# Layer one's outward products in 512 and 384 tokens, a cut in the middle, and a margin in the scheduler

## The chip, the cores and the metric

The kernel runs on one core of a Trainium2 chip. The metric is the device time of one execution in microseconds (us); lower is better. Before the change three runs gave 1051.30, 1053.89 and 1055.59 us, so the median is 1053.89 us.

## The reference

Sigmoid attention feeds two feed-forward layers over 1792 tokens (4 batches of 448), with 768 channels and 2048 hidden values:

```python
scores = scale * np.matmul(q, k.transpose(0, 1, 3, 2)) - np.log(S)   # 4 x 12 heads x 448 x 64
attn = 1.0 / (1.0 + np.exp(-scores))
x = np.matmul(attn, v)                       # to (1792, 768)

h = x @ w_in                                 # layer one: 768 -> 2048
g = np.maximum(h, 0.0) ** 2
x = g @ w_out                                # 2048 -> 768

h = x @ w_in2                                # layer two
g = np.maximum(h, 0.0) + alpha * np.minimum(h, 0.0)
out = g @ w_out2
```

## The kernel before

A first stage computes the attention (lines 290 to 480). The change does not touch it; its end is at about 159 us in the trace. What follows are the two layers, and everything below is about them.

**Units.** A layer's work is cut into units `(layer, p, fp)`: `p` is one of two pairs of batches (a pair is `PAIR = 896` tokens, side 0 the first 448, side 1 the last 448), and `fp` one of eight blocks of 256 hidden values (two halves `j` of 128). There are 16 units per layer, 32 in all, and they run one after the other. I number them 0 to 31; units 0 to 15 are layer one. The trace shows a unit every 27 to 30 us.

**Split numbers.** A float32 value is held as a high part and a low part (type fp32r), and each product of two such values takes three matmuls: high x high, high x low, low x high.

**A unit's inward half** (`product`, `add_inward`) computes the hidden values from x. Seven products `k = 0..6` of sums of blocks take the place of eight; each is nine matmuls of 128 x 448 into one PSUM bank of three (`BANK`). The first matmul of `k = 0` is cut in two at a column that goes through 32, 64, ... 416 with the unit's number, so the unit has 64 inward matmuls. VectorE (DVE) and ScalarE (ACT) take each bank out: DVE adds it to a running sum (L667), ACT applies the activation and writes the high part of g, DVE subtracts to get the low part (L659). Side 1 of g comes from `k = 3, 4`, side 0 from `k = 5, 6`.

**A unit's outward half** (`out_product`, `add_outward`) multiplies g with w_out. In layer one an output is a channel block `c` (six) by a side `t` (two); the weights stand in the array and 448 tokens of g stream past them: 12 outputs x 2 halves `j` x 3 = 72 matmuls of 448. Two outputs of one side make a pair, which fills one of the two double banks `two[0]`, `two[1]`; side 1 comes first (`for t in (1, 0)`). When a pair is done, DVE adds its 2 x 448 columns to the accumulator `acc` in SBUF (L727; for `fp == 0` ACT copies them instead, L725). A pair can start only when the pair before the last has been taken out. In layer two g stands in the array and 384 channels of w_out stream: 84 matmuls of 384.

**Other work.** DVE, ACT and GpSimd (POOL) also split the weights (L241, L630), sum and split x for the next layer (L258, L262, L265: x sums, high parts, low parts) and turn the float64 weights into float32 words (L191, L193, L203). SyncE (SP) starts the DMAs.

**What sets the order.** All work of the two layers is given as jobs to a planner (`Plan`): engine, estimated duration, what it reads and writes, and whether it uses the port that DVE and POOL share (`port=True`). `run` plays the jobs through a model of the engines and hands each engine's instructions out in that order; on the chip every engine keeps to it. TensorE's (PE's) order is fixed as written. Every other job has a due time, worked out backwards from the PE job that needs it. When an engine is free, `choose` takes the earliest due job that is ready, except that it waits for a job `s` that is due earlier and will be ready before the candidate's end, if the candidate's end falls after `due[s]`.

Of the kernel before, what the change touches and what calls it, by code (L numbers as in the profile page):

```python
# [16 lines left out]
P = 128  # L17


class Plan:  # L20
# [3 lines left out]


    HOP = 0.10
    AFTER_OWN = {"ACT": 0.12, "POOL": 0.05}
    TAIL = {"PE": 0.17, "DVE": 0.085, "ACT": 0.095, "POOL": 0.04}

# [16 lines left out]
    def run(self):  # L46
        jobs, n = self.jobs, len(self.jobs)
        after = [[] for _ in jobs]
        for j, job in enumerate(jobs):
            for i in job[3]:  # L50
                after[i].append(j)

        def length(j):
            return jobs[j][1] if jobs[j][0] != "SP" else jobs[j][5] / 0.28e6 + 2.0

        at, due, pe = 0.0, [0.0] * n, [j for j in range(n) if jobs[j][0] == "PE"]
        for j in pe:
            due[j] = at
            at += jobs[j][1]
        for j in reversed(range(n)):  # L60
            late = min((due[s] - self.HOP for s in after[j]), default=at + 50.0) - length(j) - self.TAIL.get(jobs[j][0], 0.0)
            due[j] = min(due[j], late) if jobs[j][0] == "PE" else late
        left = [len(job[3]) for job in jobs]
        ready = [0.0] * n
        engines = ("PE", "DVE", "ACT", "POOL", "SP")
        free = dict.fromkeys(engines, 0.0)
        waiting = {e: [] for e in engines}
        next_pe = 0
        port_free = dma_free = 0.0
        for j in range(n):  # L70
            if not left[j]:
                waiting[jobs[j][0]].append(j)
        order = []

        def begin(j, t):
            t = max(t, ready[j])
            return max(t, port_free) if jobs[j][4] else t

        def choose(e):
            queue = waiting[e]  # L80
            if e == "PE":
                queue = [j for j in queue if j == pe[next_pe]]
            if not queue:
                return None
            t = max(free[e], min(begin(j, free[e]) for j in queue))
            now = sorted((j for j in queue if begin(j, free[e]) <= t + 1e-9), key=lambda j: due[j])
            soon = [j for j in queue if begin(j, free[e]) > t + 1e-9]
            for j in now:
                end = t + jobs[j][1]
                if not any(due[s] < due[j] and begin(s, free[e]) < end and end > due[s] for s in soon):  # L90
                    return t, j
            s = min(soon, key=lambda j: begin(j, free[e]))
            return begin(s, free[e]), s

        while len(order) < n:
            t, j, e = min((*c, e) for e in engines if (c := choose(e)))
            engine, us, emit, before, port, size = jobs[j]
            waiting[e].remove(j)
            if e == "PE":
                next_pe += 1  # L100
            free[e] = t + us
            end = t + us + self.TAIL.get(e, 0.0)
            if port:
                port_free = t + us
            if e == "SP" or size:
                dma_free = max(dma_free, t + 0.1) + size / 0.28e6
                end = dma_free + 2.0
            order.append((t, j))
            for s in after[j]:
                left[s] -= 1  # L110
                ready[s] = max(ready[s], t + us + self.AFTER_OWN.get(e, 0.0) if jobs[s][0] == e and e != "SP" else end + self.HOP)
                if not left[s]:
                    waiting[jobs[s][0]].append(s)
        self.span = free["PE"]
        for t, j in sorted(order):
            jobs[j][2]()
# [3 lines left out]
def fused_kernel(ctx: ExitStack, tc: tile.TileContext, q, k, v, w1i, w1o, w2i, w2o, alpha, out):  # L120
# [124 lines left out]
    def values_of(p):  # L245
        return acc[p].rearrange("p (c t s) -> p c t s", c=NC, t=2)
# [23 lines left out]
    with tc.manual_schedule():  # L270
# [231 lines left out]
        OPERAND = (0, 4, 3, 5, 6, 1, 2)  # L502
        HIGH, LOW = ((0, 0), (0, 1)), ((1, 0),)
        CELL = 64
        CUT = 32

        def product(n, k):

            ps = hb[BANK[k]][:, :S]
            at_col = [0, CUT * (1 + n % (S // CUT - 1)), S] if k == 0 else [0, S]  # L510
            for c in range(KH):
                at = OPERAND[k] * HALF + c * P
                for i, (wp, xp) in enumerate(((0, 0), (0, 1), (1, 0))):
                    ends = at_col if (c, i) == (0, 0) else [0, S]
                    for a, e in zip(ends, ends[1:]):
                        nc.tensor.matmul(ps[:, a:e], W[:, wp, at:at + P], X[k][:, xp, c, a:e], start=(k < 3 and c == 0 and i == 0 and a == 0), stop=(c == KH - 1 and i == 2), skip_group_check=True)  # L516

# [6 lines left out]
        def sides(n, o):  # L524

            if UNITS[n][0] == 0:
                return [o[1]]
            return [t for t in range(2) if o[0] * P < (t + 1) * S and (o[0] + 1) * P > t * S]

        def out_product(n, o, ps, j, ways, begin, end):  # L530

            for i, (gi, wi) in enumerate(ways):
                if UNITS[n][0] == 0:
                    c, t = o
                    ops = WO[j][:, wi, c * P:(c + 1) * P], G[j][:, gi, t * S:(t + 1) * S]
                else:
                    m, e = o
                    ops = G[j][:, gi, m * P:(m + 1) * P], WO[j][:, wi, e * HALF:(e + 1) * HALF]
                nc.tensor.matmul(ps, *ops, start=(begin and i == 0), stop=(end and i == len(ways) - 1), skip_group_check=True)  # L539

        def part_of(n, os):
            layer, p, fp = UNITS[n]
            if layer == 0:
                c, t = os[0]
                cells = [((c + i) * 2 + t) * S // CELL + k for i in range(2) for k in range(S // CELL)]
                return values_of(p)[:, c:c + 2, t], cells
            m = os[0][0]
            return acc[p][:, m * DM:(m + 1) * DM].rearrange("p (e c) -> p e c", e=2), [m * DM // CELL + k for k in range(DM // CELL)]

# [26 lines left out]
        def pool(cols):  # L576
            return 0.13 + 0.0023 * cols

        PE_IN, PE_OUT = 0.2027, (0.2027, 0.1740)
        BYTES = 4 * P  # L580

        def cells_of(p, name, c):
# [78 lines left out]
        def add_inward(n):  # L661

            def bank(b):
                return hb[b][:, :S]

            def total(to, b, other, key, other_key):
                add("DVE", dve(S), lambda: nc.vector.tensor_add(to, bank(b), other), [("h", b), other_key], [key])  # L667

            for k in range(7):
                reads = [("w", OF_STEP[k], i) for i in range(2)] + [key for c in range(KH) for key in x_keys(k, c)]  # L670
                b = BANK[k]
                add("PE", 9 * PE_IN, lambda k=k: product(n, k), reads, [("h", b)])
                if k == 0:
                    add("ACT", act(S), lambda: nc.scalar.activation(e21, bank(0), AF.Copy), [("h", 0)], ["e21"])
                elif k == 1:
                    total(e12, 1, e21, "e12", "e21")
                elif k == 2:
                    total(e22, 2, e21, "e22", "e21")
                elif k == 3:
                    total(e22, 1, e22, "e22", "e22")  # L680
                    add_hidden(n, e22, "e22", e22, "e22", 1, 1)
                elif k == 4:
                    total(e12, 2, e12, "e12", "e12")
                    add_hidden(n, e12, "e12", e12, "e12", 0, 1)
                elif k == 5:
                    add_hidden(n, bank(0), ("h", 0), e11, "e11", 0, 0)
                else:
                    total(e21, 1, e21, "e21", "e21")
                    add_hidden(n, e21, "e21", e21, "e21", 1, 0)
# [3 lines left out]
        def add_outward(n):  # L693

            layer, p, fp = UNITS[n]
            size = HALF if layer else S
            pairs = []
            for os in outputs(n):
                pairs.append((os, at_pair[0] % 2))
# [2 lines left out]
            def keys(o, j, ways):  # L702
                return [("g", j, t, gi) for gi, _ in ways for t in sides(n, o)] + [key for _, wi in ways for key in ([("wo", j, 0)] if wi == 0 else [("wo", j, 1, e) for e in range(2)])]

            def products(os, b, i, j, ways, begin, end):
                add("PE", len(ways) * PE_OUT[layer], lambda: out_product(n, os[i], two[b][:, i, :size], j, ways, begin, end), keys(os[i], j, ways), [("o", b)])

            for os, b in pairs[:2]:
                for i in range(2):
# [1 line left out]
            for at, (os, b) in enumerate(pairs):  # L711
# [8 lines left out]
                        products(os, b, i, 1, HIGH + LOW, False, True)  # L720
                part, cells = part_of(n, os)
                cells = [("acc", p, cell) for cell in cells]
                both = two[b][:, :, :size]
                if fp == 0:
                    add("ACT", act(2 * size), lambda part=part, both=both: nc.scalar.activation(part, both, AF.Copy), [("o", b)], cells)  # L725
# [89 lines left out]
```

## Time and profile before

| | |
|---|---|
| three runs | 1051.30, 1053.89, 1055.59 us |
| profiled execution | 1051.43 us, of which the trace's span is 1049.6 us |
| PE busy | 1039.2 us, 99% of the span, 5639 matmuls |
| DVE, ACT, POOL busy | 746.3 us (71%), 595.6 us (57%), 256.6 us (24%) |
| inward matmuls (L516) | 2048, of which 64 are the halves of cut ones |
| outward matmuls (L539) | 1152 of 448 columns (layer one), 1344 of 384 (layer two) |

PE's busy time counts a matmul from its start to its modelled end, and matmuls overlap: one of 448 columns is listed with 366 ns, but the next starts about 203 ns after it. So the pace is read from starts: the start of a run of equal matmuls, the start of the next run, and the count between them. In the timeline view consecutive instructions of one line are merged into one row (with the shape of the first), and a row carries in brackets how long the engine stood idle before it and what ended that.

### The profile page before, as it was taken

What the parts mean: (1) busy time and instruction counts of PE and PEld (TensorE: products, weight loads), DVE (VectorE), ACT (ScalarE), POOL (GpSimd) and SP (SyncE); (2) the same over time, 40 slices, a digit from 0 to 9 for tenths busy, and PEclk for the clock granted to TensorE, in tenths of its full rate; (3) what the DMA queues carried; (4) which work ended last, traced back from release to release, by engine and by line L of the source; (5) the groups of instructions that cost most, each with busy time, mean ns of one, the idle gap of its engine ahead of it and who ended that gap; (6) DMA issues with size and microseconds to landing.
All of it is one profiled execution on the core that took longest, in us unless ns stands there. A gap on an engine that the chain in (4) does not pass through costs nothing.

```text
span 1049.6 us, 14891 instructions
## 1 busy us (share of the span) xinstructions
PE 1039.2 (99%) x5639; PEld 916.3 (87%) x5639; DVE 746.3 (71%) x990; ACT 595.6 (57%) x933; POOL 256.6 (24%) x229
## 2 busy tenths in 40 slices
PE   9999999999999999999999999999999999999998
PEld 6555548999999989899999998999999999999998
DVE  5555986698777785877777867777667656777765
ACT  4567777776666557556665675444443463343432
POOL 0001233263321152633111324432111211111110
PEclk9999999999999999999999999999999999999999
DMA  7577737666665676757677844333115611111103
GB/s 148 143 192 195 202 113 290 212 234 219 216 215 184 255 271 224 253 182 241 229 253 233 323 155 145 110 97 112 57 50 212 225 61 61 61 61 60 51 10 106
DMA packets 126007, 174.78 MB, mean 167 GB/s; under 512 B 55536, under 2 KB 98800, under 8 KB 124272
## 3 DMA queue, kind: packets, MB, share of 16 engines
q1 hardware_dynamic: 123440, 172.59, 50.6%
q10 hardware_dynamic: 2496, 1.25, 0.4%
q8 instruction: 44, 0.72, 0.3%
q14 instruction: 27, 0.22, 0.1%
HBM read 123.87 MB, written 49.94 MB: 166 GB/s over the span
## 4 chain that ended last, share of the span: by engine, by line
PE 94%; DVE 4%; issue 1%; DMA 1%; ACT 0%; SPq 0%; DVEq 0%; ACTq 0%
PE o L539 42%; PE h L516 39%; PE av L371 5%; PE sc L351 4%; DVE acc L727 1%; PE tp L318 1%; PE scr L361 1%; PE av L379 1%; DVE wi L241 1%; PE tp L321 1%; DVE x L265 1%; DMA raw<-in_moe_w_in_dram 1%; DVE g L659 0%; PE busy L395 0%; PE tp L319 0%
## 5 line engine op out<-in xcount | busy, mean ns | idle before, releaser
L516 PE MATMUL h<-x,wi 128*128 128x448 f32 (+2 forms) x2048 | 417.5, 363 | 0.5 <-DVE c L667 0.5
L516 PEld LDWEIGHTS h<-x,wi 128*128 128x128 f32 x2048 | 380.5, 188 | 32.2 <-DVE c L667 1.2
L539 PE MATMUL o<-g,wo 128*128 128x448 f32 x1152 | 238.4, 366 | 1.2 <-DVE acc L727 1.2
L539 PE MATMUL o<-wo,g 128*128 128x384 f32 x1344 | 237.0, 335 | 2.1 <-DVE g L659 1.6
L539 PEld LDWEIGHTS o<-wo,g 128*128 128x128 f32 x1344 | 233.6, 188 | 3.9 <-DVE g L659 2.3
L539 PEld LDWEIGHTS o<-g,wo 128*128 128x128 f32 x1152 | 216.0, 188 | 21.0 <-DVE acc L727 2.5
L630 POOL TENSOR_TENSOR wo<-words_o,wo 128x384 fp32r<-128x384 f32 x128 | 129.6, 1042 | 415.7 <-ACT wo L633 413.8
L727 DVE TENSOR_TENSOR acc<-o,acc 128x768 f32<-128x768 f32 (+1 forms) x182 | 184.5, 1016 | 62.8 <-PE o L539 62.4
L667 DVE TENSOR_TENSOR c<-h,c 128x448 f32<-128x448 f32 x160 | 99.5, 622 | 129.3 <-PE h L516 125.5
L633 ACT ACTIVATE wo<-words_o 128x768 fp32r<-128x768 f32 x64 | 50.7, 839 | 155.0 <-PE o L539 128.0
L659 DVE TENSOR_TENSOR g<-c,g 128x448 fp32r<-128x448 f32 x128 | 82.4, 652 | 15.2 <-ACT c L649 12.0
L353 ACT ACTIVATE a<-sc,bias 128x896 f32<-128x896 f32 x72 | 69.1, 1004 | 35.6 <-PE av L371 22.6
L265 POOL TENSOR_TENSOR stage<-acc,stage 128x448 fp32r<-128x448 f32 x36 | 45.3, 1260 | 160.9 <-ACT stage L262 160.9
L237 ACT ACTIVATE wi<-sums 128x768 fp32r<-128x768 f32 x64 | 53.5, 838 | 51.2 <-PE h L516 48.3
L191 ACT ACTIVATE raw<-raw 128x768 f32<-128x768 f32 x64 | 57.7, 904 | 37.0 <-DMA raw<-in_moe_w_out_dram 27.0
L241 DVE TENSOR_TENSOR wi<-sums,wi 128x768 fp32r<-128x768 f32 x64 | 65.4, 1023 | 10.3 <-ACT wi L237 9.4
L258 POOL TENSOR_TENSOR acc<-acc 128x448 f32<-128x448 f32 x40 | 58.4, 1465 | 10.1 <-DMA acc<-late 8.3
L371 PE MATMUL av<-a,v 128*64 128x448 f32 x288 | 59.4, 548 | 0.0
L193 ACT ACTIVATE raw<-raw 128x768 int32<-128x768 uint32 x64 | 57.2, 898 | 0.0
L655 ACT ACTIVATE pos<-c 128x448 f32<-128x448 f32 x48 | 27.7, 578 | 50.4 <-DVE c L667 49.7
L241 DVE TENSOR_TENSOR wi<-words_i,wi 128x768 fp32r<-128x768 f32 (+1 forms) x64 | 52.6, 823 | 3.5 <-ACT wi L237 3.1
L657 DVE SCALAR_TENSOR_TENSOR c<-c,nal,pos 128x448 f32<-128x448 f32 x64 | 44.4, 693 | 9.1 <-ACT c L656 8.9
(75 smaller groups left out, 850.3 us busy)
## 6 DMA issues: line engine op xcount, KB each, us to landing
raw<-in_moe_w_in_dram SPq DMA_DIRECT2D x32, 768.0 KB, 5.9
raw<-in_moe_w_out_dram SPq DMA_DIRECT2D x32, 768.0 KB, 5.3
kept_x<-stage SPq DMA_DIRECT2D x36, 448.0 KB, 3.9
x<-kept_x SPq DMA_DIRECT2D x12, 1344.0 KB, 11.0
v<-in_v_dram SPq DMA_DIRECT2D x24, 192.0 KB, 2.9
nat<-in_q_dram SPq DMA_DIRECT2D x22, 192.0 KB, 3.4
nat<-in_k_dram SPq DMA_DIRECT2D x20, 192.0 KB, 3.3
late<-held SPq DMA_DIRECT2D x12, 224.0 KB, 2.2
```

The source lines that it names most:

```text
L191: nc.scalar.activation(half.bitcast(F32), half.bitcast(F32), AF.Prelu, scale=2.0 ** -112, alpha=2.0 ** 32)
L193: nc.scalar.activation(half, half.bitcast(U32), AF.Copy, scale=2.0 ** -29 * (1 - 2.0 ** -12), bias=-0.5 + 7.5 * 2.0 ** -12)
L241: nc.vector.tensor_sub(lo, w, hi)
L258: eng.tensor_sub(to, x, y)
L353: nc.scalar.activation(sig[u, j], ps[:, :, :S], AF.Sigmoid, bias=bias[:, :1], scale=SCALE)
L371: nc.tensor.matmul(avs[u][h * D:(h + 1) * D, :S], vals[u][:, h, j, :], a[:, h, :], start=(u % 2 == 0 and j == 0), stop=(u % 2 == 1 and j = ...
L516: nc.tensor.matmul(ps[:, a:e], W[:, wp, at:at + P], X[k][:, xp, c, a:e], start=(k < 3 and c == 0 and i == 0 and a == 0), stop=(c == KH - 1 ...
L539: nc.tensor.matmul(ps, *ops, start=(begin and i == 0), stop=(end and i == len(ways) - 1), skip_group_check=True)
L630: nc.gpsimd.tensor_sub(WO[j][:, 1, at], words["o"][:, j, at], WO[j][:, 0, at])
L659: add("DVE", dve(S), lambda: nc.vector.tensor_sub(gl, e, gh), [key, h_key], [l_key], port=True)
L667: add("DVE", dve(S), lambda: nc.vector.tensor_add(to, bank(b), other), [("h", b), other_key], [key])
L727: add("DVE", dve(2 * size), lambda part=part, both=both: nc.vector.tensor_add(part, both, part), [("o", b), *cells], cells)
```

## The change

Four edits, all in the two layers:

- **Outward products of layer one.** An output's token range is no longer side 0 or side 1 but `TOKENS = (0:512, 512:896)`. An output of `t = 1` streams 384 tokens, all of them in side 1; one of `t = 0` streams 512, which are all of side 0 and the first 64 of side 1. The 72 matmuls of a unit become 36 of 384 and 36 of 512; the order (t = 1 first) stays. DVE's add (or ACT's copy) of a pair becomes 2 x 384 or 2 x 512 columns. `sides` tells the planner which sides of g an output reads.
- **The cut.** The first matmul of a unit is cut at column 224 in every unit.
- **The margin.** In `choose` a job now also gives way if its end falls after `due[s] - MARGIN`, with `MARGIN = 1.0` us.
- **The planner's costs.** Outward matmuls are costed by their columns: 0.1740 us for 384 and 0.2270 us for 512 (before 0.2027 for 448).

```diff
     HOP = 0.10
+    MARGIN = 1.0
...
-                if not any(due[s] < due[j] and begin(s, free[e]) < end and end > due[s] for s in soon):
+                if not any(due[s] < due[j] and begin(s, free[e]) < end and end > due[s] - self.MARGIN for s in soon):
...
-        CUT = 32
-
-        def product(n, k):
+        TOKENS = (slice(0, 512), slice(512, PAIR))
+
+        def product(k):
...
-            at_col = [0, CUT * (1 + n % (S // CUT - 1)), S] if k == 0 else [0, S]
...
-                    ends = at_col if (c, i) == (0, 0) else [0, S]
+                    ends = [0, S // 2, S] if (k, c, i) == (0, 0, 0) else [0, S]
...
-                return [o[1]]
+                return [1] if o[1] else [0, 1]
...
-                    ops = WO[j][:, wi, c * P:(c + 1) * P], G[j][:, gi, t * S:(t + 1) * S]
+                    ops = WO[j][:, wi, c * P:(c + 1) * P], G[j][:, gi, TOKENS[t]]
...
-                cells = [((c + i) * 2 + t) * S // CELL + k for i in range(2) for k in range(S // CELL)]
-                return values_of(p)[:, c:c + 2, t], cells
+                at = TOKENS[t]
+                cells = [((c + i) * PAIR + k) // CELL for i in range(2) for k in range(at.start, at.stop, CELL)]
+                return acc[p].rearrange("p (c s) -> p c s", c=NC)[:, c:c + 2, at], cells
...
-        PE_IN, PE_OUT = 0.2027, (0.2027, 0.1740)
+        PE_IN, PE_OUT = 0.2027, {384: 0.1740, 512: 0.2270}
...
+            def size_of(os):
+                return HALF if layer else TOKENS[os[0][1]].stop - TOKENS[os[0][1]].start
+
             def products(os, b, i, j, ways, begin, end):
-                add("PE", len(ways) * PE_OUT[layer], lambda: out_product(n, os[i], two[b][:, i, :size], j, ways, begin, end), keys(os[i], j, ways), [("o", b)])
+                size = size_of(os)
+                add("PE", len(ways) * PE_OUT[size], lambda: out_product(n, os[i], two[b][:, i, :size], j, ways, begin, end), keys(os[i], j, ways), [("o", b)])
```

Since the planner's costs, token ranges and rule change, the order on DVE, ACT, POOL and SP changes from the first units on. In the pieces below a name is the tile written, then the tiles read (numbers tell buffers apart): o_1794 and o_1798 are the two double banks, h the inward banks, g_1790 and g_1791 the hidden values of `j = 0` and `j = 1`, acc the accumulators. Lines stand one to five higher in the changed kernel: its L732 is the L727 of before, L660 is L659, L242 is L241, L266 is L265.

PE, the end of unit 4 and the start of unit 5, before:

```order
L539 MATMUL o_1798<-g_1790,wo_1788 128x448 x3
L539 MATMUL o_1798<-g_1791,wo_1789 128x448 x3
L516 MATMUL h_1795<-x_70,wi 128x192
L516 MATMUL h_1795<-x_70,wi 128x256
L516 MATMUL h_1795<-x_70,wi 128x448 x8
L516 MATMUL h_1796<-x_71,wi 128x448 x9
```

and the same place in the changed kernel:

```order
L539 MATMUL o_1798<-g_1790,wo_1788 128x512 x3
L539 MATMUL o_1798<-g_1791,wo_1789 128x512 x3
L516 MATMUL h_1795<-x_70,wi 128x224 x2
L516 MATMUL h_1795<-x_70,wi 128x448 x8
L516 MATMUL h_1796<-x_71,wi 128x448 x9
```

The count and order of matmuls stay; the widths of the outward ones and of the cut one change.

DVE in the outward half of unit 7, where x for the next pair is also being made (L265), before:

```order
L659 TENSOR_TENSOR g_1790<-c_1785,g_1790 128x448
L265 TENSOR_TENSOR x_74<-acc_1792,x_74 128x448
L727 TENSOR_TENSOR acc_76<-o_1794,acc_76 128x2x448
L659 TENSOR_TENSOR g_1791<-c_1782,g_1791 128x448
L727 TENSOR_TENSOR acc_76<-o_1798,acc_76 128x2x448
L265 TENSOR_TENSOR x_74<-acc_1792,x_74 128x448 x2
L727 TENSOR_TENSOR acc_76<-o_1794,acc_76 128x2x448
L727 TENSOR_TENSOR acc_76<-o_1798,acc_76 128x2x448
```

and in the changed kernel:

```order
L660 TENSOR_TENSOR g_1790<-c_1785,g_1790 128x448
L732 TENSOR_TENSOR acc_76<-o_1794,acc_76 128x2x384
L266 TENSOR_TENSOR x_74<-acc_1792,x_74 128x448
L732 TENSOR_TENSOR acc_76<-o_1798,acc_76 128x2x384
L660 TENSOR_TENSOR g_1791<-c_1782,g_1791 128x448
L732 TENSOR_TENSOR acc_76<-o_1794,acc_76 128x2x384
L732 TENSOR_TENSOR acc_76<-o_1798,acc_76 128x2x512
```

The two low parts of x that stood between the second and the third add of an output pair have moved behind the fourth.

DVE in the outward half of unit 11, before:

```order
L659 TENSOR_TENSOR g_1790<-c_1785,g_1790 128x448
L241 TENSOR_TENSOR wi<-words_i,wi 128x384
L727 TENSOR_TENSOR acc_1792<-o_1794,acc_1792 128x2x448
L727 TENSOR_TENSOR acc_1792<-o_1798,acc_1792 128x2x448
L659 TENSOR_TENSOR g_1791<-c_1782,g_1791 128x448
```

and in the changed kernel:

```order
L732 TENSOR_TENSOR acc_1792<-o_1794,acc_1792 128x2x384
L242 TENSOR_TENSOR wi<-words_i,wi 128x384
L732 TENSOR_TENSOR acc_1792<-o_1798,acc_1792 128x2x384
L660 TENSOR_TENSOR g_1790<-c_1785,g_1790 128x448
L660 TENSOR_TENSOR g_1791<-c_1782,g_1791 128x448
```

Here the low part of g that the first product of `t = 0` needs (g_1790, side 0) has moved behind two adds of output pairs.

## Rows read from the trace of the kernel before

**Rows 1.** The page: engine PE, granted clock by slices, shares of the last-ended chain

```profile
PE 1039.2 (99%) x5639; PEld 916.3 (87%) x5639; DVE 746.3 (71%) x990; ACT 595.6 (57%) x933; POOL 256.6 (24%) x229
...
PEclk9999999999999999999999999999999999999999
...
PE 94%; DVE 4%; issue 1%; DMA 1%; ACT 0%; SPq 0%; DVEq 0%; ACTq 0%
```

**Rows 2.** Timeline of PE, unit 6: start, length, engine, work, count

```profile
325.14 12.94 PE L516 MATMUL h<-x,wi 128*128 128x224 f32 x64
337.92 14.76 PE L539 MATMUL o<-g,wo 128*128 128x448 f32 x72
352.51 0.79 PE L516 MATMUL h<-x,wi 128*128 128x256 f32 x4
```

**Rows 3.** Timeline of PE, unit 3

```profile
241.88 13.22 PE L516 MATMUL h<-x,wi 128*128 128x128 f32 x64
254.94 15.04 PE L539 MATMUL o<-g,wo 128*128 128x448 f32 x72
269.81 0.41 PE L516 MATMUL h<-x,wi 128*128 128x160 f32 x2
```

**Rows 4.** Timeline of PE, inward half of unit 13

```profile
520.36 13.03 PE L516 MATMUL h<-x,wi 128*128 128x32 f32 x64
533.22 14.75 PE L539 MATMUL o<-g,wo 128*128 128x448 f32 x72
```

**Rows 5.** Timeline of PE, inward half of unit 19

```profile
688.83 12.94 PE L516 MATMUL h<-x,wi 128*128 128x224 f32 x64
701.62 14.75 PE L539 MATMUL o<-wo,g 128*128 128x384 f32 x84
```

**Rows 6.** Timeline of PE, outward half of unit 16 (layer two)

```profile
616.35 14.73 PE L539 MATMUL o<-wo,g 128*128 128x384 f32 x84
630.91 0.41 PE L516 MATMUL h<-x,wi 128*128 128x160 f32 x2
```

**Rows 7.** Timeline of PE, units 7, 9, 10, 15, 17, 18: rows with idle time before them

```profile
365.30 9.89 PE L539 MATMUL o<-g,wo 128*128 128x448 f32 x48
375.54 5.22 PE L539 MATMUL o<-g,wo 128*128 128x448 f32 x24 [0.35 <-DVE acc L727]
380.60 0.61 PE L516 MATMUL h<-x,wi 128*128 128x288 f32 x3
...
431.74 5.18 PE L539 MATMUL o<-g,wo 128*128 128x448 f32 x24 [0.50 <-DVE acc L727]
...
444.75 5.74 PE L516 MATMUL h<-x,wi 128*128 128x448 f32 x27 [0.48 <-DVE c L667]
...
598.32 5.13 PE L539 MATMUL o<-g,wo 128*128 128x448 f32 x24 [0.33 <-DVE acc L727]
...
651.26 0.62 PE L539 MATMUL o<-wo,g 128*128 128x384 f32 x2 [0.49 <-ACT g L658]
653.00 7.75 PE L539 MATMUL o<-wo,g 128*128 128x384 f32 x43 [1.12 <-DVE g L659]
...
681.27 7.73 PE L539 MATMUL o<-wo,g 128*128 128x384 f32 x43 [0.52 <-DVE g L659]
```

**Rows 8.** Timeline of POOL and DVE in unit 7, before PE's wait

```profile
371.34 4.16 POOL L265 TENSOR_TENSOR x<-acc,x 128x448 fp32r<-128x448 f32 x3 [14.30 <-ACT x L262]
371.37 3.11 DVE L265 TENSOR_TENSOR x<-acc,x 128x448 fp32r<-128x448 f32 x2
...
374.41 2.08 DVE L727 TENSOR_TENSOR acc<-o,acc 128x896 f32<-128x896 f32 x2
```

**Rows 9.** Groups by form: DVE's add of a layer-two pair (busy, mean ns, idle)

```profile
L727 DVE TENSOR_TENSOR acc<-o,acc 128x768 f32<-128x768 f32 x98 | 93.5, 955 | 39.8 <-PE o L539 39.8
```

**Rows 10.** Timeline of PE and DVE, outward half of unit 11

```profile
477.77 14.76 PE L539 MATMUL o<-g,wo 128*128 128x448 f32 x72
...
479.88 0.62 DVE L659 TENSOR_TENSOR g<-c,g 128x448 fp32r<-128x448 f32 x1
```

More of the change, by code (lines that the diff above doesn't have):

```diff
@@ L671, in add_inward @@
                 b = BANK[k]
-                add("PE", 9 * PE_IN, lambda k=k: product(n, k), reads, [("h", b)])
+                add("PE", 9 * PE_IN, lambda k=k: product(k), reads, [("h", b)])
                 if k == 0:
@@ L695, in add_outward @@
             layer, p, fp = UNITS[n]
-            size = HALF if layer else S
             pairs = []
@@ L722, in add_outward @@
                 cells = [("acc", p, cell) for cell in cells]
+                size = size_of(os)
                 both = two[b][:, :, :size]
```

## The prediction

> **What bounds the kernel now.** I read the page first. PE is busy for 99% of the span, and the chain that ended last is PE for 94% [rows 1]. So there is no engine to unload; time can only come from PE's own pace, from its few waits, or from matmuls that cost more than they need. The granted clock is at its upper level, 2.4 GHz, in every slice, so the clock is no term. The mean duration of a matmul hides its pace, so I went on to the timeline of PE and divided starts by counts, unit by unit. Three things come out.
>
> First, the same 448-column matmul has two paces. In unit 6 the 72 outward ones take 352.51 − 337.92 = 14.59 us, 202.6 ns each [rows 2]; in unit 3 they take 269.81 − 254.94 = 14.87 us, 206.5 ns each, with no idle time noted [rows 3]. The pace holds through a whole unit, inward half too: 13.06 us in unit 3 against 12.78 in unit 6. I call the second pace held. Of the 32 units, 3, 5, 8, 12 and 16 are held in their inward half and 3, 5, 8 and 12 in their outward one (unit 16's outward matmuls have 384 columns). What starts or ends it lies at the cut: unit 6 follows a held unit and unit 19 follows 384-column matmuls, both are cut at 224, and both go at the fast pace [rows 2, 5]. These are the only two units with that cut.
>
> Second, the place of the cut costs time by itself. Among fast units the inward half is 12.78 us with the cut at 224 [rows 2] and 533.22 − 520.36 = 12.86 with the cut at 32 [rows 4], with the other cuts between, the more the farther from the middle.
>
> Third, PE stands idle at seven places, 0.33 to 1.12 us each, 3.79 us together [rows 7]. A place costs more than its idle time: unit 7's outward half is 380.60 − 365.30 = 15.30 us, 0.71 over unit 6, for 0.35 us of idle. With 0.3 us more for each, the seven cost about 6 us. Four wait for DVE to empty a PSUM bank, three for a part of g. In unit 7 the reason can be seen: two low parts of x on DVE take 3.11 us, 1.6 each, while three of the same operation run on POOL, and the add that PE waits for starts behind them at 374.41 [rows 8].
>
> **The change part by part.**
>
> *The cut.* In the cycle of 13 cuts the mean distance from column 224 is 103 columns; the cut at 32, 192 columns away, costs 0.08 us. In proportion the mean is 0.043 us a unit, times 32 units: **−1.4 us**. Nothing hides or replaces it, since it is PE's own time.
>
> *The held pace.* If the cut at 224 gives the fast pace in every unit, as in its two cases, five inward halves lose 63 x 3.9 ns = 0.25 us each, and four outward halves 0.28 us: **−2.35 us**. Bounds: held everywhere costs 27 more inward halves, +6.7 us; never held is the value taken.
>
> *512 and 384 for 448 and 448.* 36 matmuls of each width replace 72, in 16 units: 576 pairs. The 384-column one is in the trace, though in layer two with another operand streaming: (630.91 − 616.35) / 84 = 173.3 ns [rows 6]. No row shows 512. Its columns at 2.4 GHz are 213.3 ns. The 384-column one takes 13.3 ns above its columns (160.0), the fast 448-column one 15.9 above its 186.7, the held one 19.8. With the 384's surplus 512 would take 226.7; on the line through 384 and fast 448 it takes 231.9; on the line through 384 and held 448, 239.7. The planner's own cost table says 227.0, which no row supports. I take 229, between the first two, as 12 of the 16 outward halves of layer one go at the fast pace: 173.3 + 229 = 402.3 against 405.2 for two fast ones, 2.9 ns x 576 = **−1.7 us**. Bounds: −3.0 us at 226.7, none at 231.9, +4.5 us at 239.7.
>
> The formula of the Trainium skill (TensorE: Matmul & The Clock Gate, section Back-to-back issue gap) is columns / 2.4 plus a fixed 2.5 ns. By it the two halves cost the same for any split, 378.3 ns a pair, and this edit would give nothing; the trace does not agree with its size, 173.3 against its 162.5 for 384 columns and 202.6 against 189.2 for 448, and the surplus grows with the columns.
>
> *Shorter pairs and DVE.* A pair of 384 frees its double bank sooner but leaves less time: between the end of the first pair and the start of the third PE has 8 matmuls, 8 x 173.3 = 1.39 us, for DVE's add of 768 columns, 0.96 us [rows 9]. Layer two already runs so, and the waits that it has are for g, not for this add [rows 7]. For 512 the add grows to 0.955 x 1024 / 768 = 1.27 us beside 12 x 229 = 2.75 us of matmuls. Nothing here if DVE is free in time. The total of columns that DVE adds is unchanged.
>
> *Less cover for side 0 of g.* The t = 1 products run while side 0 of g is still made. They now last 36 x 173.3 = 6.24 us, not 36 x 202.6 = 7.29. In unit 11 the low part that the first t = 0 product needs is ready at 480.50, and that product starts at 477.77 + 7.29 = 485.06 [rows 10]: 4.6 us in hand, of which 1.05 go. By position alone that is free. But the new order uses the rest up: this low part now stands behind two adds. The second add cannot end before the second pair does (24 matmuls, 4.16 us) plus about 1.2 us, the low part takes 0.62, and a POOL operation that holds the port first adds up to 1.2: ready 6.0 to 7.2 us into the half, against 6.24 for the first t = 0 product and 6.7 for its third matmul, the one that reads the low part. So 0 to 0.5 us here; behind it on DVE stand the other low part and the third add, which the pair after next waits for.
>
> *The margin and the new order.* At unit 7 the two DVE operations that delayed the add have moved behind the fourth add; at unit 15, the same place in the other pair, one of two remains; at units 9 and 10 the weight work between the operations that empty banks is gone or shortened; at unit 17 a weight split has moved behind the low parts of g. That is where about 5 of the 6 us stand. The rule does this in general: it asks 1.0 us of distance, close to what one POOL operation adds to a DVE one. Against it, holding DVE idle pushes the less urgent work together, and places such as unit 11 appear. Bounds: all 6 us gone, or 3 us more than now (a 0.5 us wait with its 0.3 in four more units). I take 3.5 us gone and 1.0 new: **−2.5 us**.
>
> *Sum.* −1.4 − 2.35 − 1.7 − 2.5 = −7.95 us. The profiled execution took 1051.43 us, 1.83 outside its span: 1043.5. It lies 2.46 us under the median of 1053.89, near the lowest of three runs. What differs between executions must be waits or paces, since the work is the same, and part of that goes too, so I carry 1.0 of the 2.46: **1044.5 us**.
>
> **The rivals.**
>
> *Only columns count.* 512 + 384 cost what two 448 do, and waits move instead of going. The cut and the held pace remain: −3.75, 1047.7 by the profiled execution, about 1048.7 as a median. For it: a straight line is the simplest reading of two widths. Against it: the order has cleared the very places that waited.
>
> *Cover lost.* The earlier need of side 0 and the idling DVE give back what the other edits save: waits of 0.5 us plus 0.3 in about seven more units, +5.6, and none of the old gone, against −5.45 from cut, pace and width: no change, about 1052. For it: unit 11's order. Against: most units keep 3 us or more of room.
>
> *The held pace everywhere (slower).* The pace is settled at the passage from outward to inward matmuls. If 512-column matmuls leave PE in the state that holds, and run held themselves at 239.7, then inward +6.7, outward +4.5 − 1.1, cut −1.4, waits −2.5: +6.2, about 1058. With 512 at 239.7 and the other terms as above, 4.5 − 1.1 − 1.4 − 2.5 = −0.5 us is left, so it turns slower once more than seven inward halves are held. For it: the five held units all follow 448-column outward matmuls of layer one, the part that changes. Against: the cut at 224 was fast after both kinds of predecessor.
>
> **How the numbers follow.** Forecast 0.58 (1040 to 1048.5), only columns 0.22 (1046 to 1051), cover lost 0.12 (1049 to 1055), held everywhere 0.08 (1054 to 1061). About 0.5%, 5.3 us, is what can be told from no change here, so faster means under 1048.6 us: 0.93 x 0.58 + 0.45 x 0.22 + 0.03 x 0.12 = 0.64; slower means over 1059.2: 0.3 x 0.08, with something for a wait that I have not seen: 0.06; the same 0.30. The range leaves out the upper part of the last two cases and a little below: 1039.5 to 1052.5.
>
> **What would show it.** Cut: fast inward halves of 12.78 us in all units. Pace: 202.6 ns inward everywhere; one unit near 206.5 contradicts it. Width: starts 226 to 232 ns apart for 512, 173 for 384 also with g streaming. Waits: no idle in units 7, 9, 10 and 15, less in 17, perhaps some in 11. Wrong would be: 512 at 235 or more, a held inward half after the 224 cut, or idle places that add up to more than 6 us.

## The result, and the profile after

Four runs of the changed kernel gave 1042.98 to 1044.28 us, median 1043.16; four of the kernel before, beside them, 1051.30 to 1055.59, median 1052.96. The ratio is 0.9907, with a 95% interval of 0.9884 to 0.9930: 0.9% faster, within 1.4 us of the forecast of 1044.5. A profile with a span of 1041.2 us belongs to the execution of 1042.99 us, so the two profiled executions differ by 8.44 us. By the starts of PE's matmuls the two layers went from 886.13 to 877.72 us, 8.41 less; the attention stage and the tail changed by half a microsecond each, in opposite directions.

The page of the changed kernel, to be laid beside [rows 1]:

```profile
PE 1032.3 (99%) x5639; PEld 906.4 (87%) x5639; DVE 740.5 (71%) x990; ACT 599.3 (58%) x933; POOL 256.5 (25%) x229
...
PEclk9999999999999999999999999999999999999999
...
PE 93%; DVE 3%; DMA 2%; ACT 1%; issue 1%; SPq 0%; DVEq 0%; ACTq 0%
```

As many matmuls as before, the same clock, and PE is still what bounds the kernel: it is busy for less time, not better covered.

PE in unit 6, then the end of that unit from inside its 512-column matmuls (the answers to [rows 2]; columns: start, length, engine, work, count):

```profile
323.33 12.95 PE L516 MATMUL h<-x,wi 128*128 128x224 f32 x64
336.12 14.63 PE L539 MATMUL o<-g,wo 128*128 128x384 f32 x72
350.59 12.95 PE L516 MATMUL h<-x,wi 128*128 128x224 f32 x64
...
344.69 6.06 PE L539 MATMUL o<-g,wo 128*128 128x512 f32 x26
350.59 0.38 PE L516 MATMUL h<-x,wi 128*128 128x224 f32 x2
```

The inward half is 336.12 − 323.33 = 12.79 us, and so it is in all 32 units of this trace but unit 0 (12.90, it follows the attention stage) and unit 16 (13.38, a wait). No half is held, where five inward and four outward ones were. The outward half is 14.47 us, 401.9 ns for a 384 and a 512 together, where two fast matmuls of 448 took 405.2. Inside, the 512-column ones start (350.59 − 344.69) / 26 = 226.9 ns apart (the starts are rounded to 0.01 us, so 226.5 to 227.3).

Unit 19, in layer two, for [rows 5, 6]:

```profile
680.48 12.94 PE L516 MATMUL h<-x,wi 128*128 128x224 f32 x64
693.26 14.75 PE L539 MATMUL o<-wo,g 128*128 128x384 f32 x84
707.84 0.38 PE L516 MATMUL h<-x,wi 128*128 128x224 f32 x2
```

12.78 and 14.58 us: a unit that was cut at 224 before and did not wait is what it was.

All rows of PE in the two layers that have idle time before them (for [rows 7]; the last bracket is the idle time and what ended it):

```profile
175.84 10.58 PE L539 MATMUL o<-g,wo 128*128 128x384 f32 x48 [0.20 <-ACT acc L730]
228.83 12.64 PE L539 MATMUL o<-g,wo 128*128 128x384 f32 x60 [0.26 <-DVE g L660]
602.15 7.57 PE L516 MATMUL h<-x,wi 128*128 128x448 f32 x36 [0.32 <-DVE c L668]
644.61 7.74 PE L539 MATMUL o<-wo,g 128*128 128x384 f32 x43 [0.35 <-DVE g L660]
672.89 7.75 PE L539 MATMUL o<-wo,g 128*128 128x384 f32 x43 [0.63 <-DVE g L660]
```

The idle rows of units 7, 9, 10 and 15 are gone; 17 and 18 still wait for a part of g; units 0, 2 and 16 are new. Units 3, 9 and 11 have no idle row, but their outward halves are 0.13 to 0.26 us longer than 14.47. DVE in unit 7, where the two parts of x had stood before the third add [rows 8]:

```profile
367.62 0.63 DVE L266 TENSOR_TENSOR x<-acc,x 128x448 fp32r<-128x448 f32 x1 [0.30 <-ACT x L263]
368.17 0.95 DVE L732 TENSOR_TENSOR acc<-o,acc 128x768 f32<-128x768 f32 x1
369.03 0.62 DVE L660 TENSOR_TENSOR g<-c,g 128x448 fp32r<-128x448 f32 x1
369.84 0.96 DVE L732 TENSOR_TENSOR acc<-o,acc 128x768 f32<-128x768 f32 x1 [0.19 <-PE o L539]
372.60 1.22 DVE L732 TENSOR_TENSOR acc<-o,acc 128x1024 f32<-128x1024 f32 x1 [1.81 <-PE o L539]
```

Before the last two adds the wait has turned round: now DVE waits for PE, and the add of 1024 columns takes 1.22 us (the prediction worked out 1.27).

### The profile page after: what moved, and what is told of

It is laid out like the page before. It is cut to its first block, busy times and chain, and to the rows that moved or that the text cites. A ratio compares the mean times of both kernels' runs of the same rounds, so it can differ in the third digit from the quotient of the medians.

```text
span 1041.2 us, 14883 instructions
## 1 busy us (share of the span) xinstructions
PE 1032.3 (99%) x5639; PEld 906.4 (87%) x5639; DVE 740.5 (71%) x990; ACT 599.3 (58%) x933; POOL 256.5 (25%) x229
## 4 chain that ended last, share of the span: by engine, by line
PE 93%; DVE 3%; DMA 2%; ACT 1%; issue 1%; SPq 0%; DVEq 0%; ACTq 0%
PE o L539 43%; PE h L516 37%; PE av L372 4%; PE sc L352 4%; PE tp L319 1%; PE scr L362 1%; PE av L380 1%; PE tp L322 1%; DVE g L660 1%; DVE acc L732 1%; DMA nat<-in_q_dram 1%; DMA raw<-in_moe_w_in_dram 1%; DMA raw<-in_moe_w_out_dram 0%; ACT wi L238 0%; DVE wi L242 0%
## 5 line engine op out<-in xcount | busy, mean ns | idle before, releaser
L516 PE MATMUL h<-x,wi 128*128 128x448 f32 (+1 forms) x2048 | 414.7, 362 | 0.3 <-DVE c L668 0.3
L539 PE MATMUL o<-g,wo 128*128 128x512 f32 (+1 forms) x1152 | 235.2, 363 | 0.5 <-DVE g L660 0.3
L539 PEld LDWEIGHTS o<-g,wo 128*128 128x128 f32 x1152 | 208.2, 188 | 24.2 <-DVE g L660 0.9
L732 DVE TENSOR_TENSOR acc<-o,acc 128x768 f32<-128x768 f32 (+1 forms) x182 | 184.6, 1015 | 61.4 <-PE o L539 60.8
L660 DVE TENSOR_TENSOR g<-c,g 128x448 fp32r<-128x448 f32 x128 | 83.8, 665 | 20.4 <-ACT c L650 17.3
L266 POOL TENSOR_TENSOR stage<-acc,stage 128x448 fp32r<-128x448 f32 x36 | 47.2, 1311 | 174.8 <-ACT stage L263 174.8
L242 DVE TENSOR_TENSOR wi<-sums,wi 128x768 fp32r<-128x768 f32 x64 | 62.7, 984 | 8.7 <-ACT wi L238 8.1
L242 DVE TENSOR_TENSOR wi<-words_i,wi 128x768 fp32r<-128x768 f32 (+1 forms) x64 | 51.0, 799 | 4.1 <-ACT wi L238 4.0
```

The source lines that it names most:

```text
L242: nc.vector.tensor_sub(lo, w, hi)
L660: add("DVE", dve(S), lambda: nc.vector.tensor_sub(gl, e, gh), [key, h_key], [l_key], port=True)
L732: add("DVE", dve(2 * size), lambda part=part, both=both: nc.vector.tensor_add(part, both, part), [("o", b), *cells], cells)
```

## The experiments

The theory is the prediction's: four savings that add up, a cut in the middle that costs less and ends the held pace, cheaper widths, and fewer waits. The main rivals: the 512-column matmuls before it, and not the cut, make the inward half fast; and the waits went by one of the edits alone. Each group has its own runs of the kernel before beside it: median 1052.33 us for the first four, 1052.52 for the next four, 1052.67 for the last four. Ratios carry their 95% intervals.

**The cut alone** (in the kernel before):

```diff
-            at_col = [0, CUT * (1 + n % (S // CUT - 1)), S] if k == 0 else [0, S]
+            at_col = [0, S // 2, S] if k == 0 else [0, S]
```

> The kernel before with the cut at column 224 in every unit, nothing else; the order on all engines is that of before. Theory A (the predecessor decides): a matmul width whose pace lies on a fixed grid (384 and 512 columns) hands over to the inward half always in the same phase, and any cut then leads to the fast pace, while after fast 448-column outward matmuls the phase drifts and some units of layer one stay held at 206.7 ns. Then only the cut's own cost goes, -1.4 us, and a few of units 1 to 16 are still held (inward 13.03 us): about 1051.0 to 1052. Theory B (the cut at 224 decides, as the prediction said): all 32 inward halves 12.78 us, no outward half of 14.87, -3.75 us, about 1049.

Median 1050.63 us, ratio 0.9981 [0.9972, 0.9991]. PE from the wait in unit 3 on, and from unit 11's:

```profile
261.41 10.18 PE L539 MATMUL o<-g,wo 128*128 128x448 f32 x48 [0.86 <-DVE acc L727]
271.43 12.94 PE L516 MATMUL h<-x,wi 128*128 128x224 f32 x64
284.21 14.76 PE L539 MATMUL o<-g,wo 128*128 128x448 f32 x72
298.80 12.96 PE L516 MATMUL h<-x,wi 128*128 128x224 f32 x64
...
473.43 5.83 PE L516 MATMUL h<-x,wi 128*128 128x448 f32 x27 [0.53 <-DVE c L667]
479.10 15.04 PE L539 MATMUL o<-g,wo 128*128 128x448 f32 x72
493.98 12.94 PE L516 MATMUL h<-x,wi 128*128 128x224 f32 x64
```

The two inward halves after the wait are 284.21 − 271.43 = 12.78 and 12.79 us, fast. After the wait inside unit 11 the outward half is held, 493.98 − 479.10 = 14.88 us, and the next unit is fast again: the cut in the middle ends a held pace. Every inward half of this trace starts fast, whether held 448-column matmuls stand before it (units 4, 8 and 12), fast ones, or the 384-column ones of layer two. But only 1.7 us of the 3.75 arrive. PE's idle rows add up to 5.24 us in this trace, 1.45 more than before; 0.86 of that is the wait in unit 3. That a faster PE runs into the old order of DVE fits this, but is not shown: only one execution of the kernel before is traced, and the kernel before without its cuts, which is no faster, has a wait of 0.86 us in unit 3 too.

**New widths with the old cuts and no margin** (in the changed kernel):

```diff
-    MARGIN = 1.0
+    MARGIN = 0.0
...
-                    ends = [0, S // 2, S] if (k, c, i) == (0, 0, 0) else [0, S]
+                    ends = [0, 32 * (1 + n % (S // 32 - 1)), S] if (k, c, i) == (0, 0, 0) else [0, S]
```

> The changed kernel with the margin at 0 and the cut going through 32 to 416 as before: the 512 and 384 tokens alone. Theory A: no unit is held in its inward half whatever its cut, since 512 or 384 columns stand before each; inward 12.78 to 12.87 by the cut, outward 14.47. -3 (width) - 1.1 - 1.2 (pace) = about -5.5 us, 1047.5, with the waits of before. Theory B: about five units with cuts away from 224 are held (13.03 to 13.1), 1048.7.

Median 1046.17 us, ratio 0.9941 [0.9926, 0.9956]. Units 13 and 14:

```profile
515.71 13.28 PE L516 MATMUL h<-x,wi 128*128 128x32 f32 x64
528.82 14.61 PE L539 MATMUL o<-g,wo 128*128 128x384 f32 x72
543.27 13.02 PE L516 MATMUL h<-x,wi 128*128 128x64 f32 x64
556.12 14.61 PE L539 MATMUL o<-g,wo 128*128 128x384 f32 x72
```

Unit 13 is held (13.11 us; a fast half with its cut is 12.86), and 512-column matmuls stand right before it. Units 5 and 10 are held too. So the rival that the width alone makes the pace fast fell: a cut at some other column can start the held pace even after 512. With the next run, which differs from this one in the cut alone, the cut is worth 2.4 us here: about 1.3 for its place and 0.75 for three held halves.

**No margin** (in the changed kernel, `MARGIN = 0.0` alone):

> The changed kernel with the margin at 0. If the margin took the waits away, they come back: +2.5 us, about 1045.7, with idle time of DVE origin in units 7, 9, 10 or 15. Rival: the new widths alone changed the order so far that the waits are gone without the margin: 1043.2, as the changed kernel.

Median 1043.74 us, ratio 0.9920 [0.9905, 0.9935], 0.6 us above the changed kernel, with overlapping intervals. The waits in 7, 10 and 15 are gone here as well, and in the run before this one, so the new widths, with their costs in the planner, cleared them; no run separates the widths from the costs. The one long wait is in unit 9; DVE, POOL and PE there:

```profile
423.50 1.93 DVE L242 TENSOR_TENSOR wi<-sums,wi 128x768 fp32r<-128x768 f32 x1
424.69 3.23 POOL L259 TENSOR_TENSOR acc<-acc 128x448 f32<-128x448 f32 x2
425.35 1.55 DVE L660 TENSOR_TENSOR g<-c,g 128x448 fp32r<-128x448 f32 x1
426.82 0.94 DVE L732 TENSOR_TENSOR acc<-o,acc 128x768 f32<-128x768 f32 x1
426.96 3.24 PE L539 MATMUL o<-g,wo 128*128 128x512 f32 x13 [1.74 <-DVE g L660]
```

The low part of g (L660) takes 1.55 us instead of 0.62 while POOL works, and PE waits 1.74 us for it; the weight split before it (L242) takes 1.93 us where the same operation elsewhere takes 0.96. The add behind it (L732) is not slowed beside the same POOL work: 0.94 us. The Trainium skill says why the two differ (SBUF — State Buffer, section Who interferes with whom): a DVE instruction contends with GpSimd's reads when both its inputs lie in SBUF, as L660's do, and not with one of them, as in L732, whose other input is in PSUM. The trace agrees on both sides. One more thing is in this trace: unit 4's inward half, cut in the middle, starts fast and turns held after its 37th matmul, with no idle row (12.89 us). So the cut settles how a half starts; it doesn't rule out a change inside it.

**No cut** (in the changed kernel):

```diff
-                    ends = [0, S // 2, S] if (k, c, i) == (0, 0, 0) else [0, S]
+                    ends = [0, S]
```

> The changed kernel with the unit's first matmul whole: 63 inward matmuls; the order on all other engines is that of the changed kernel. Theory A and B: without a cut nothing frees the pace, all 32 inward halves run held at 206.7 ns, 63 x 206.7 = 13.02 us against 12.79: +7.5 us, about 1050.5. Rival: the cut only costs (18 ns a unit) and the pace is fast in any case: -0.6 us, 1042.6.

Median 1047.06 us, ratio 0.9951 [0.9934, 0.9968]. A unit of each layer:

```profile
323.58 12.93 PE L516 MATMUL h<-x,wi 128*128 128x448 f32 x63
336.35 14.61 PE L539 MATMUL o<-g,wo 128*128 128x384 f32 x72
...
709.68 13.18 PE L516 MATMUL h<-x,wi 128*128 128x448 f32 x63
722.69 14.73 PE L539 MATMUL o<-wo,g 128*128 128x384 f32 x84
```

Layer one, whose inward halves follow 512-column matmuls, is fast without a cut (12.77 us); layer two, where they follow 384-column ones, is held (13.01; in units 18 and 19 only up to a wait of 0.5 us that is new). That is half of what was expected of a kernel without the cut, 3.9 us of 7.5: in layer one the new width does the cut's work.

**The margin alone** (in the kernel before, the change's two lines in `choose`):

> The kernel before with the margin of 1.0 us in the scheduler, nothing else. If the margin is what clears the waits (about 6 us in the kernel before), about half goes: -3 us, 1049.3, with no idle of DVE origin in units 7, 9, 10, 15. Rival: the margin only moves them; the changed kernel lost its waits through the widths and costs of the outward matmuls: 1052.3, idle time elsewhere but of the same sum.

Median of ten 1048.31 us, ratio 0.9965 [0.9954, 0.9975]: 4.2 us by the medians, 3.7 by the ratio, where 3 were expected. The ten go from 1046.95 to 1051.09, and the profiled one is the slowest, so its trace doesn't show which waits went in the typical execution. In that slowest one units 9 and 10 have no idle row any more, 7 and 15 still wait (0.26 and 0.28 us), units 2 and 3 wait 0.7 us each, and six inward halves are held.

**480 and 416 tokens** (in the changed kernel):

```diff
-        CELL = 64
-        TOKENS = (slice(0, 512), slice(512, PAIR))
+        CELL = 32
+        TOKENS = (slice(0, 480), slice(480, PAIR))
...
-        PE_IN, PE_OUT = 0.2027, {384: 0.1740, 512: 0.2270}
+        PE_IN, PE_OUT = 0.2027, {384: 0.1740, 416: 0.1880, 480: 0.2170}
```

> The changed kernel with the tokens cut at 480 instead of 512 (and the planner's bookkeeping in cells of 32 instead of 64 columns, its costs 0.217 and 0.188 us). Theory A, what is above the columns' 2.4 GHz time is 13.3 ns for multiples of 128 columns only: 416 and 480 carry 16 to 20 ns as 448 does, 189 to 193 and 216 to 220 ns, 405 to 413 a pair against 400.0 for 384 + 512: +2.9 to +7.5 us, 1046 to 1050.7. Theory B, it grows with the columns (13/12 of them): 187.8 + 216.7 = 404.4, +2.5 us, 1045.7, and 512 at 226.7 would be the odd one. Theory C, it is 13.3 ns for every width but 448: 400.0, no change.

Median 1042.28 us, ratio 0.9904 [0.9889, 0.9919]. From inside the 480-column matmuls of a unit to its end, and the outward half of the unit before from its start on:

```profile
308.83 14.70 PE L539 MATMUL o<-g,wo 128*128 128x416 f32 x72
...
317.31 6.23 PE L539 MATMUL o<-g,wo 128*128 128x480 f32 x28
323.37 0.79 PE L516 MATMUL h<-x,wi 128*128 128x224 f32 x4
```

Here 480 columns take (323.37 − 317.31) / 28 = 216.4 ns and the half 323.37 − 308.83 = 14.54 us, 0.07 more than with 512 and 384, or 1.1 us in 16 units. With the starts rounded to 0.01 us that is 216 to 217 ns, as theory B has it and the low end of A; 416 columns take about 187 ns, which is C's figure. So none of the three gives both widths; the pair, 403.9 ns, is nearest to B's 404.4. Yet the time is not longer, as it was in A and B, since PE waits less: only one idle row is left in the layers, 0.35 us, and units 17 and 18 have none.

**The cut in layer two only** (in the changed kernel), run twice:

```diff
-                    ends = [0, S // 2, S] if (k, c, i) == (0, 0, 0) else [0, S]
+                    ends = [0, S // 2, S] if (k, c, i) == (0, 0, 0) and n > NU // 2 else [0, S]
```

> The changed kernel with the cut only in units 17 to 31, where 384-column matmuls of layer two stand before the inward half; whole in units 0 to 16. From the kernel without any cut: inward 12.768 and outward 14.445 us in layer one, 12.781 and 14.586 in layer two, all fast. Theory (the predecessor's width decides whether a cut is needed): 17 x 0.018 + 15 x 0.022 = -0.6 us, about 1042.5. Rival: the cut in layer one also shields against held stretches after waits: some units of layer one at 13.0 or 14.6, 1043.2 or more.

> The changed kernel with the cut in units 17 to 31 alone, on the same chip as the changed kernel: 0.6 us below it by the matmuls' starts (17 x 0.018 + 15 x 0.022). Rival: no difference, since what PE saves it waits.

Medians 1042.44 and 1042.61 us, ratios 0.9906 [0.9891, 0.9921] and 0.9905 [0.9892, 0.9919]. In the second the changed kernel ran on the same chip (below): 1042.98. The starts do show what an uncut half saves in layer one:

```profile
322.74 12.93 PE L516 MATMUL h<-x,wi 128*128 128x448 f32 x63
335.50 14.61 PE L539 MATMUL o<-g,wo 128*128 128x384 f32 x72
```

12.76 to 12.77 us against 12.79: 0.02 a unit, some 0.6 us in all with what the outward halves save, and too little for the time to tell, as runs of one kernel differ by over 1 us.

**The kernel before without its cuts** (`ends = [0, S]`):

> The kernel before with the unit's first matmul whole. Theory: without a cut the pace carries over from one half to the next as long as widths stay the same, so layer one is fast or held in long stretches that only waits end, and after 384-column matmuls every inward half of layer two is held: 15 x 0.23 = +3.5, less 32 x 0.061 = -2.0 for the cuts, and in layer one between -2.2 (never held) and +6.5 (always held): 1051.5 to 1060. Rival: the cut in the kernel before is only a cost: -2.0 us, 1050.3, no new held units.

Median 1053.36 us, ratio 1.0013 [0.9997, 1.0028]: the cycle of cuts was worth nothing that can be told. Units 10 and 11:

```profile
444.20 5.84 PE L516 MATMUL h<-x,wi 128*128 128x448 f32 x27 [0.56 <-DVE c L667]
449.89 15.04 PE L539 MATMUL o<-g,wo 128*128 128x448 f32 x72
464.77 7.60 PE L516 MATMUL h<-x,wi 128*128 128x448 f32 x36
472.76 5.74 PE L516 MATMUL h<-x,wi 128*128 128x448 f32 x27 [0.39 <-DVE c L667]
478.34 14.78 PE L539 MATMUL o<-g,wo 128*128 128x448 f32 x72
```

After the wait at 444.20 the outward half is held (14.88 us), and so is the start of unit 11; after the next wait the rest of unit 11 is fast. With 448 columns throughout, a wait can start the held pace and a wait can end it, and in between it carries over from unit to unit.

**The changed kernel once more**, beside the last three:

> The changed kernel itself, beside the three others on the same chip: 1043.2 us.

Median 1042.98 us, ratio 0.9909 [0.9895, 0.9922]. Its trace has the first one's waits in units 2, 16, 17 and 18, but none in 0 and 11, whose outward halves take 14.46 us.

**Cut and margin with the old widths** (in the kernel before, the edits of the cut alone and of the margin alone together):

> The kernel before with the cut at 224 and the margin, and 448-column outward matmuls as before. If the two gains add up: -1.9 - 4.0 = -5.9 us, about 1046.6. If the cut alone gained only half of its 3.75 us because PE at the faster pace ran into waits, and the margin clears these: -3.75 - 4.0, about 1044.8. If both gains are partly the same one (held stretches that waits start): -4.5, about 1048.

Median 1045.10 us, ratio 0.9928 [0.9915, 0.9940]: −7.6 us, more than −1.7 and −4.2 together, though at the edge of the intervals (the two ratios multiplied give 0.9946). PE's idle rows add up to 2.20 us, against 5.24 with the cut alone: waits ate part of its saving, and with the margin most of them are gone. Units 7, 9 and 10 have none; 15, 17 and 18 still wait, 0.27 to 0.48 us. The five runs lie within 1.0 us.

**480 and 416 with the cut in layer two only** (both edits above):

> The tokens cut at 480, the first matmul cut only in units 17 to 31. Before an inward half of layer one stand 480-column matmuls, whose pace of 216.7 ns is 32.5 steps of 6.67 ns, not a whole number as 173.3 (26) and 226.7 (34) are. If the whole number of steps is what lets 512-column matmuls hand over to the fast pace without a cut, some units of layer one are held here: inward 13.0 us, up to 16 x 0.24 = +3.8. If only the equality of widths matters (a held pace needs 448 before it or 384), none is: 0.6 us below the 480-column kernel with all cuts, 1041.7.

Median 1043.56 us, ratio 0.9909 [0.9894, 0.9924]. Outward half of unit 11, then units 12 and 13:

```profile
473.16 14.84 PE L539 MATMUL o<-g,wo 128*128 128x416 f32 x72
487.84 13.18 PE L516 MATMUL h<-x,wi 128*128 128x448 f32 x63
500.86 14.80 PE L539 MATMUL o<-g,wo 128*128 128x416 f32 x72
515.50 13.18 PE L516 MATMUL h<-x,wi 128*128 128x448 f32 x63
```

The uncut halves of units 1 to 11 are fast. Unit 11's outward half is delayed by 0.15 us, with no idle row, and from there on the inward halves are held at 13.02 us to the end of layer one. The outward halves between them are slower too, 14.64 us for 14.53, since 416 columns take 190 ns there. So a held pace passes through 480-column matmuls. With 512-column ones before them the uncut halves of units 1 to 15 were fast in all three traces that have them, also behind outward halves with waits. That 480's pace is not a whole number of steps fits, but no run tells this from another property of that width.

No version is faster than the changed kernel by more than a run of it differs from the next: the best ratio is that of 480 and 416, 0.9904 against 0.9907.

## Why the prediction was right, step by step

**The cut, −1.4 us.** It came nearly as worked out: inward halves of 12.78 to 12.79 us, and no distance from the middle left to pay. The 25 inward halves of before that were neither held nor delayed put the cost of the cycle at 1.3 us.

**The held pace, −2.35 us.** Also as worked out, about 1.2 from five inward halves and 1.15 from four outward ones. The rival of a held pace everywhere had the right place, the passage from outward to inward matmuls, and the wrong sign: 512-column matmuls leave PE fast. In layer one the cut is therefore not needed (no cut: fast there), in layer two it is. That the cut at 224 is fast after any predecessor rested on two units; the cut alone shows it for the start of every half. The prediction had the pace start and end at the cut alone; that was too narrow, as waits do both (the kernel before without its cuts).

**The widths, −1.7 us.** 14.592 − 14.467 = 0.125 us in 16 units, −2.0. The pair came out at 401.9 ns for 402.3 forecast, but not for the reason given, so that the size fits is luck. The step that failed is the reading that the surplus grows with the columns: 512 has 384's surplus, 226.9, whose pair with 173.3 would be 400.2. The 1.7 ns that remain (36 pairs: 0.06 us a unit) lie in the first matmuls after each change of width, about 0.03 us at the start of the half and 0.04 where 384-column matmuls give way to 512-column ones. "Only columns count" is ruled out by the starts.

**The waits, −2.5 us.** What the halves take beyond the undelayed ones went from about 6.7 to 4.0 us, −2.7: 0.5 in inward halves, 0.7 in layer one's outward ones, 1.5 in layer two's. Two misses made this sum, and that they nearly cancel is luck. The prediction let 3.5 us go and 1.0 arrive; 4.8 went, and about 2.1 us came, nearly all in units 0, 2, 3, 9, 11 and 16, most of them at places not named ahead. It also gave the margin and the new order one sum, as though both were needed. The runs tell them apart:

| widths | cut | margin | ratio to before |
|---|---|---|---|
| 448, 448 | 224 | none | 0.9981 [0.9972, 0.9991] |
| 448, 448 | cycle | 1.0 | 0.9965 [0.9954, 0.9975] |
| 448, 448 | 224 | 1.0 | 0.9928 [0.9915, 0.9940] |
| 512, 384 | cycle | none | 0.9941 [0.9926, 0.9956] |
| 512, 384 | 224 | none | 0.9920 [0.9905, 0.9935] |
| 512, 384 | 224 | 1.0 | 0.9907 [0.9884, 0.9930] |

On top of the cut, the margin is worth 0.9928 / 0.9981, about 0.5%, with the old widths and 0.9907 / 0.9920, about 0.1%, with the new ones, which lies within the intervals. The new widths are worth 0.6% without the margin and 0.2%, 2.1 us, with it, which is the size of the width term. So either of the two clears most of the old waits of layer one, and the second adds little; in unit 9 it is the margin that removes the wait for g that the widths leave. What stays open is how the margin alone gains 4.2 us: the one trace of it is not of a typical execution.

**Less cover in unit 11.** 0 to 0.5 us were forecast. PE and DVE there, for [rows 10]:

```profile
472.57 14.76 PE L539 MATMUL o<-g,wo 128*128 128x384 f32 x72
487.17 1.19 PE L516 MATMUL h<-x,wi 128*128 128x224 f32 x6
...
476.96 0.96 DVE L732 TENSOR_TENSOR acc<-o,acc 128x768 f32<-128x768 f32 x1
477.83 1.98 DVE L660 TENSOR_TENSOR g<-c,g 128x448 fp32r<-128x448 f32 x2
```

The two low parts end 479.81 − 472.57 = 7.2 us into the half and the first of them, slowed beside POOL, at 6.7, just when the third t = 0 matmul wants it. The half is 487.17 − 472.57 = 14.60 us for 14.47: 0.13 us. In the second trace of the changed kernel the first low part ends 6.5 us into the half, and the half takes 14.46 us. "Cover lost" had this place right and its number wrong, since most other units kept their room.

**The sum.** −1.3 − 2.35 − 2.0 − 2.7 = −8.35 us, of −8.41 by the starts, against −7.95 forecast. The 1.0 us by which the median was to lie above the profiled execution was too much: it lies 0.17 above. These two misses, 0.5 and 0.8 us, are why the forecast came out 1.3 us too high. The reason given, that waits and held units differ from execution to execution, fits the spread of the runs (1.3 us for the changed kernel, 4.3 for the one before), but is not shown: the kernel before has one trace.

## What to carry to other kernels

Where one engine is busy for 99% of the span, divide starts by counts, unit by unit: two paces of one instruction hide in an average and in a duration. Make a saving on the engine that bounds together with room in the order of the engine that feeds it; the cut alone brought 1.7 us, the margin alone 4.2, the two together 7.6. Before crediting one of several edits with a wait that has gone, take each away from the whole, since two may clear the same one.

## What the runs showed of the hardware that was not expected

- The starts of equal matmuls are 173.3 ns apart for 384 columns, about 187 or 190 for 416, 202.6 or 206.5 for 448, about 216.5 for 480 and 226.9 for 512, all at a granted clock of 2.4 GHz. Above the columns at that clock that is some 13 ns for 384 and 512, 13 or 17 for 416, 16 or 20 for 448, and 16 to 17 for 480: it does not grow evenly with the columns.
- At 448 columns there are two paces, and at 416 too. The held one lasts: from a cut to the next unit's cut in the kernel before, and from a wait to the next wait, 28 us later, in the kernel before without cuts. A cut in the middle ended it each time. Behind 384-column matmuls an uncut half was held each time, behind 512-column ones never, and 480-column ones carry it on. Cuts at other columns gave now one pace and now the other. What in the engine holds the pace, no run shows.
- A cut at the middle costs 0.02 us a unit, one 192 columns away 0.1: cutting a matmul is nearly free if its halves are equal.
